# A planner's prices for TensorE, SyncE and shared VectorE/GpSimd time, and the instruction order that follows from them

## The chip, the cores and the metric

One core of a Trainium2 chip runs the whole program: TensorE (PE in the rows), VectorE (DVE), ScalarE (ACT), GpSimd (POOL), SyncE (SP, which here issues nearly all transfers) and 16 DMA engines. The metric is the device time of one execution in microseconds, the median of a few runs.

## The reference

Causal attention with a bias from cumulative sums, then two feed-forward blocks, all in fp32:

```python
scores = scale * np.matmul(q, k.transpose(0, 1, 3, 2))      # 4 x 8 heads, 576 x 576, depth 64
bias = -(cum[:, :, :, None] - cum[:, :, None, :])           # cum = cumsum(max(s, 0))
scores = np.where(causal, -1e9, scores + np.minimum(bias, 0.0))
...                                                         # softmax, then times v
x = attn_out  ->  2304 x 512
g = s * max(x @ w_in, 0) ** 2 + b                           # 512 -> 2048
x = g @ w_out                                               # 2048 -> 512
h = max(x @ w1, x @ w2, x @ w3)                             # 512 -> 768
out = h @ w_fin                                             # 768 -> 512
```

## The kernel before, in words

Attention is done in 20 jobs, one pair of heads each. Jobs 0 to 3 do the first 320 query rows of batch 0 (part "A"), 4 to 7 the other 256 rows of it ("B"), and jobs 8 to 19 a whole pair of heads ("W", 576 rows). A job is a chain of small steps: the scores of a block of query rows (`qk`, L571 and L573; in W jobs `qk_set`, L581, one head j at a time), their row minima on VectorE (`least`, L592), the exponential on ScalarE (`expo`, L598), its transposition on TensorE (`turn_p`, L670) and a copy out of PSUM (`copy_p`, L265 or L269), the product with v (`av`, L689), and the division by the row sums (`turn_r` L618, `spread_r` L660, `x_copy` L697).

In W jobs the operands of `qk_set` lie in a tile `set` (two of them, used in turn). It is filled by `round_set` (a rounded copy of q and k, 128 x 1152, on ACT or DVE), `rest_set` (what the rounding left out, in three pieces on POOL), `again_set`, and a transfer `decay_set` (L523, four rows from `dm_d`).

The first feed-forward block's first 6 of 16 hidden blocks run in the same stretch: the matmuls `mm` of L276 to L278 (three for each product, high and low parts) fill TensorE's time between attention steps as far as the finished jobs have given them input. Weights are converted on the way in (`weight_steps`: L301 issues the load, L306 on ACT, then L309 to L321 on DVE, ACT and POOL). From about 265 us on only feed-forward matmuls are left.

The order on every engine comes from a planner in the kernel (`Plan.order`), run as the program is built. Every step has a price per engine it may run on (`costs`), a due time (`prio`) and the steps that it needs. The planner always takes next what can begin first by its own clock; among what can begin within `SLACK` us of that, it takes the lowest due time. A step that may run on two engines goes to the second when the first would be done later than that by a margin (`LATE`, `LATE_F`, `LATE_0`). `LAND` and `FAR` are its allowances for a transfer's landing; `PORT` names DVE steps that it doesn't let overlap GpSimd's steps. What it writes down is a fixed order, in which each engine works one instruction after the other.

The step `keep` (L543) transposes the identity into a PSUM bank that nobody reads. It has the last due time of all, so that the planner puts it where TensorE would have nothing else.

Of the kernel before, what the change touches and what calls it, by code (L numbers as in the profile page):

```python
# [18 lines left out]
P = 128  # L19
BIG = 1.0e9  # L20
LO = 32
PARTS = 3
# [3 lines left out]
XS_BUFS = 2  # L26
ST2 = 3
COLD = 6.7
DM_AT = 47.138
DM_AFTER = ("dd", 2)  # L30
D_AT = -2.0
WARM = 30
KEEP = 1
KEEPS = 40
VIA = 8

WO = ((0, 1, 2), (3, 4, 5), (6, 7, 8, 9))
PACE_0 = 0
PACE_S = 1.381
F_AT = 15  # L40
F_PACE = 2.4

PER = {'A': 5.6, 'B': 9.085, 'W': 16.166}
Q_LOAD = -8.188
K_LOAD = -18.606
SET_AT = -5.4
V_LOAD = 3.528
TURN = -6.0
LEAST = 0.259
EXP = 0.52  # L50
D_T = 1.77
P_HI = 0.616
R_AT = 0.543
D_AV = 5.38
X_COPY = 0.345
X_HI = 2.019
X_LO = 2.696
AV = {"A": ((0, 1, 2),), "B": ((0, 1, 2), (3, 4)), "W": ((0, 1, 2), (3, 4))}
W_1 = -2.561
W_S1 = 3.438  # L60
W_2 = 28.48
W_S2 = 1.679
WG = (0, 1, 2, 5, 6)
WX = (7, 10, 13)
# [1 line left out]
WB_S = 8.964  # L66
WO_AT = 0.055
W_AT = (0, 2.0, 2.3, 2.8, 2.9, 3.3)
SLACK = 0.03
LATE = 0.898  # L70
LATE_F = 0.923
LATE_0 = 0.133
BUSY = 150
RATE = 1.022
RATE_D = 360e3
FAR_S = 0.306
FAR_R = 0.557
FAR_Q = 0.632
LOADED = (60, 260)
LOAD = {"ACT": RATE, "DVE": RATE}  # L80
LAND = {"wa": 1.1, "ws": 1.0, "wb": 1.1, "wf": 1.1, "q": 0.7, "k": 1.0, "v": 1.0, "decay": 0.7, "x_d": 0.7, "load_x": 0.7, "t": 1.1, "lw": 1.0, "ls": 1.0, "s_b": 0.6}
FAR = {"ws": FAR_S, "wa": FAR_S, "q": FAR_Q, "k": FAR_Q, "v": FAR_Q}
TAIL = {"least": 0.067, "inv": 0.085, "x_copy": 0.055, "relua": 0.06, "relub": 0.06, "copy_p": 0.045, "copy_r": 0.045}
MANUAL = lambda nc: {x.engine for x in (nc.tensor, nc.scalar, nc.vector, nc.gpsimd, nc.sync)}


class Plan:
# [8 lines left out]
             ("DVE", "ACT"): 0.13, ("DVE", "PE"): 0.17, ("DVE", "Pool"): 0.2, ("Pool", "PE"): 0.15, ("Pool", "DVE"): 0.15, ("Pool", "ACT"): 0.1}  # L96


    PORT = ("square", "lo", "hi", "x_hi", "x_lo", "xb_lo", "lo_h", "lo_y", "hl")
    OVERLAP = 0.1  # L100

    def __init__(self, rings):
# [10 lines left out]
    def order(self):  # L113
        n = len(self.steps)
        waits, users, needs = [0] * n, [[] for _ in range(n)], []
# [6 lines left out]
        free, start, end, engine = {}, [None] * n, [None] * n, [None] * n  # L122
# [54 lines left out]
        for i in range(n):  # L177
            if not waits[i]:
                make_ready(i)
        for done in range(n):  # L180
            best = None
            for e in ready:
                times = list(choices(e))
                if times:
                    limit = min(times)[0] + SLACK
                    b, p, i = min((x for x in times if x[0] <= limit), key=lambda x: (x[1], x[2]))
                    if best is None or b < best[0]:
                        best = (b, i, e)
            if best is None:
                raise RuntimeError(f"stuck after {done} of {n}: {[(self.steps[i][0]) for m in ready.values() for i in m][:40]}")  # L190
            t, i, e = best
            key, costs, prio, _, f, args, _, _ = self.steps[i]
            engine[i], start[i], end[i] = e, t, t + costs[e] * (2 if e == "PE" and t < COLD else LOAD.get(e, 1) if LOADED[0] < t < LOADED[1] else 1)
            free[e] = end[i] - (TAIL.get(key[0], 0) if e == "DVE" else 0)
            if has_port(i, e):
                port[e] = end[i]
            for o in costs:
                ready[o].remove(i)
            self.now = []
            for r, back in taken(i):  # L200
                z = min(range(len(held[r])), key=lambda z: given_back(held[r][z], e))
                held[r][z] = back
                self.now.append((r, z))
            for j in users[i]:
# [12 lines left out]
def fused_kernel(ctx, tc, q, k, v, s, w_in, w_out, ms, mb, w1, w2, w3, w_fin, out,  # L217
                 f_split=6):
    nc = tc.nc
    B, H, S = s.shape  # L220
# [528 lines left out]
    def add(key, engine, cost, prio, needs, f, *args, att=False, delay=None, **k):  # L749

        costs = engine if isinstance(engine, dict) else {engine: cost}
        if att and key[0] not in ("copy_rb", "load_rb", "x_copy", "x_hi", "x_lo"):
            attention.append(key)
        if engine == "SP":
            raw, kind = key[0] in ("q", "k"), key[0] + (key[1] if key[0] == "w" else "")
            plan.add(("issue", *key), {"SP": (0.6 if raw else 0.475) * cost[0] + 0.17 * (cost[0] // 3)}, prio, needs, f, *args, delay=0.65, **k)
            plan.add(key, {"DMA": 1.5 if key[0] == "s_b" else cost[1] * P * 4 / RATE_D}, prio, [("issue", *key)], lambda: None, delay=0.95 + LAND.get(kind, 0.4) + FAR.get(kind, 0) + (delay or 0))
            return
        plan.add(key, costs, prio, needs, f, *args, delay=delay, **k)
# [28 lines left out]
    for job in jobs:  # L788
# [33 lines left out]
        for x, u in enumerate(units):  # L822
            i, k0, k1, c0, c1 = UNITS[u]
            if pairs:
                same = [("turn_p", n - 1, z, j) for z in range(6) if UNITS[z][0] == i for j in range(2)]
                order = [("after", ("qk", n, units[x - 1]))] if x else [("after", z) for z in last_qk]
                ready = [("oh", n), ("q", n), ("k", n)]
                add(("qk", n, u), "PE", 5 * (k1 - k0) / 2400 + 0.25, at[u, 0], ready + [("dd", i)] + [("after", z) for z in same] + order, qk, job, u,
                    take=[("sm", [("least", n, u, j)]) for j in range(2)], **a)
            for j in range(2):  # L830
                same = [("turn_p", n - 1, z, j) for z in range(6) if UNITS[z][0] == i]
                if not pairs:
                    order = [("qk", n, units[x - 1], j)] if x else [("qk", n, units[-1], 0)] if j else last_qk
                    add(("qk", n, u, j), "PE", 2 * max(0.112, mm_cost(k1 - k0)) + 0.04, at[u, j], [("rest", n, j, z) for z in range(PARTS)] + [("again", n, j), ("decay", n, j)] + [("after", z) for z in same + order], qk_set, job, u, j,
                        take=[("sm", [("least", n, u, j)])], **a)
                add(("least", n, u, j), "DVE", dve(k1 - k0) + 0.08, at[u, j] + LEAST, [qk_key(n, u, j)] + same + ([("least", n, units[x - 1], j)] if k0 else []), least, job, u, j, **a)
        for i in job.chunks:
# [5 lines left out]
        by = lambda m: {"ACT": act_ps(m), "DVE": dve_ps(m)} if pairs else {"DVE": dve_ps(m), "ACT": act_ps(m)}  # L843
        freed = [("x_copy", n - z, hf) for z in range(1, NP + 2) for hf in range(2)]
        if spread:
            add(("turn_r", n), "PE", 0.109, end + R_AT + 0.5, [("inv", n)], turn_r, job, take=[("sm", [("copy_r", n), ("rest_r", n)])], **a)
            add(("copy_r", n), by(P), 0, end + R_AT + 0.5, [("turn_r", n)] + [("spread_r", n - 1, hf) for hf in range(2)], copy_r, job, **a)
            add(("rest_r", n), "DVE", dve_ps(P), end + R_AT + 0.5, [("copy_r", n)], rest_r, job, **a)
        else:
            add(("turn_r", n), "PE", 0.109, end + R_AT + 0.5, [("inv", n)], turn_r, job, take=[("sm", [("copy_r", n)])], **a)  # L850
            add(("copy_r", n), by(P), 0, end + R_AT + 0.5, [("turn_r", n), ("load_rb", n - 2), ("spread_r", n - 1, 0), ("spread_r", n - 2, 0)], copy_rw, job, **a)
            plan.add(("issue", "save_r", n), {"SP": 0.475 if pairs else 0.95}, end + R_AT + 0.6, [("copy_r", n)], save_r, job)
            plan.add(("save_r", n), {"DMA": 0.05}, end + R_AT + 0.6, [("issue", "save_r", n)], lambda: None, delay=1.2)
# [7 lines left out]
        for z, (u, j) in enumerate(turns):  # L861
# [6 lines left out]
                add(("turn_p", n, u, j), "PE", max(0.03, 0.109 * (c1 - c0) - 0.05), t, [("exp", n, i, j), ("pp",) if i > 2 else ("pre", "Pool")] + order, turn_p, job, u, j, take=[("sm", [("copy_p", n, u, j)])], **a)  # L868
# [7 lines left out]
                add(("copy_p", n, u, j), {"ACT": act_ps(m), "DVE": dve_ps(m)}, 0, t + P_HI, [("turn_p", n, u, j)] + over, copy_p, job, u, j, take=take, **a)  # L876

        t2 = end + D_AV
        for x, g in enumerate(job.groups):
            cost = 0.03 + sum(mm_cost(z, 4) + 0.05 for z in (HS[hf] + HN[hf] - max(c * P, HS[hf]) for c in g for hf in job.halves) if z > 0)  # L880
# [806 lines left out]
```

## Time and profile before

| | us |
|---|---|
| median of 3 runs | 876.33 (875.36 to 876.64) |
| the profiled execution | 873.61 |
| its span, first to last instruction | 871.7 |
| TensorE busy in it | 859.2 |
| VectorE, ScalarE, GpSimd busy | 642.4, 468.4, 342.5 |

The span is what the views below divide up; 1.9 us lie around it. "Busy" of TensorE counts pipelined matmuls from start to modelled end, so it shows where the engine has nothing to do, not how well it is used.

### The profile page before, as it was taken

To read this page: it belongs to the slowest core of one execution; us is meant where nothing else is said; L and a number is where in the kernel's file an instruction comes from. 1 tells how busy PE (TensorE), PEld (TensorE's weight loads), DVE (VectorE), ACT (ScalarE), POOL (GpSimd) and SP (SyncE) were. 2 spreads that over 40 slices of the span, in tenths; PEclk is the share of its full clock that TensorE was granted. 3 is DMA by queue.
4 is the path that set the end of the run, shared out by engine and by line. 5 is a ranking of instruction groups with operands and counts; after the bars stand their busy time and mean duration, and the time that the engine had idled before them with its cause. 6 is when DMAs were issued, how large, how long until landed. Compare 5 with 4: busy or idle time off the path is not lost.

```text
span 871.7 us, 15599 instructions
## 1 busy us (share of the span) xinstructions
PE 859.2 (99%) x5056; PEld 770.5 (88%) x5056; DVE 642.4 (74%) x1550; ACT 468.4 (54%) x1173; POOL 342.5 (39%) x367
## 2 busy tenths in 40 slices
PE   8999999999999999999999999999999999999998
PEld 7678888888888999999988888889999999989996
DVE  8889897989887877777979796444668366846650
ACT  7887998888883435536355452451235323432221
POOL 3334689767842322524142150420227222602220
PEclk9899999999999999999999999999999999999999
DMA  7645666676553456475859766329886255715501
GB/s 209 195 130 169 202 208 188 213 239 190 186 173 120 144 185 217 146 252 167 292 177 304 240 196 209 102 95 325 303 300 228 74 169 178 233 73 170 169 25 73
DMA packets 110672, 162.72 MB, mean 187 GB/s; under 512 B 10912, under 2 KB 61952, under 8 KB 110592
## 3 DMA queue, kind: packets, MB, share of 16 engines
q1 hardware_dynamic: 110352, 161.45, 57.2%
q8 instruction: 41, 0.67, 0.3%
q14 instruction: 39, 0.32, 0.1%
q10 hardware_dynamic: 240, 0.28, 0.1%
HBM read 117.26 MB, written 44.42 MB: 185 GB/s over the span
## 4 chain that ended last, share of the span: by engine, by line
PE 89%; DVE 5%; DMA 3%; ACT 1%; SPq 1%; issue 1%; DVEq 0%; ACTq 0%
PE mm L276 25%; PE mm L277 25%; PE mm L278 25%; PE pt L670 5%; PE px L689 4%; PE ps L581 4%; DVE pp L592 1%; PE ps L571 1%; DMA stage<-in_moe_w_out_dram 1%; DMA stage<-in_moe_w_in_dram 1%; ACT pp L598 1%; SPq L503 1%; DMA wst<-in_moe_w_in_dram 1%; DMA raw<-in_k_dram 1%; DMA set<-dm_d 0%
## 5 line engine op out<-in xcount | busy, mean ns | idle before, releaser
L272 POOL TENSOR_TENSOR gbl<-g,gbh 128x512 fp32r<-128x512 f32 (+1 forms) x50 | 64.2, 1285 | 141.2 <-ACT gbh L265 141.2
L1131 ACT ACTIVATE g<-g 128x512 f32<-128x512 f32 (+4 forms) x86 | 48.3, 561 | 81.8 <-DVE g L1127 81.3
L598 ACT ACTIVATE pp<-pp,mn 64x64 f32<-64x64 f32 (+4 forms) x160 | 88.3, 554 | 4.5 <-DVE mn L592 4.0
L272 POOL TENSOR_TENSOR set<-raw,set 64x384 fp32r<-64x384 f32 x72 | 76.4, 1084 | 30.1 <-ACT set L265 23.0
L276 PE MATMUL mm<-ty,sdp 128*128 128x384 f32 x252 | 84.2, 334 | 0.0
L277 PE MATMUL mm<-ty,sdp 128*128 128x384 f32 x252 | 84.2, 334 | 0.0
L278 PE MATMUL mm<-ty,sdp 128*128 128x384 f32 x252 | 84.2, 334 | 0.0
L1127 DVE TENSOR_SCALAR g<-mm 128x512 f32<-128x512 f32 (+4 forms) x86 | 51.7, 601 | 42.0 <-PE mm L278 41.5
L670 PE MATMUL pt<-ident,pp 128*128 128x128 f32 x480 | 78.2, 281 | 3.0 <-DVE mn L592 1.4
L278 PE MATMUL mm<-gbh,wb_out 128*128 128x512 f32 (+2 forms) x200 | 73.6, 368 | 0.0
L276 PE MATMUL mm<-gbh,wb_out 128*128 128x512 f32 (+2 forms) x200 | 73.6, 368 | 0.0
L277 PE MATMUL mm<-gbl,wb_out 128*128 128x512 f32 (+2 forms) x200 | 73.6, 368 | 0.0
L278 PE MATMUL mm<-xa,wb_in 128*128 128x512 f32 (+1 forms) x200 | 73.4, 367 | 0.0
L277 PE MATMUL mm<-xa,wb_in 128*128 128x512 f32 (+1 forms) x200 | 73.4, 367 | 0.0
L276 PE MATMUL mm<-xa,wb_in 128*128 128x512 f32 (+1 forms) x200 | 73.4, 367 | 0.0
L272 POOL TENSOR_TENSOR ga<-g,ga 128x448 fp32r<-128x448 f32 (+3 forms) x36 | 39.5, 1099 | 79.3 <-ACT ga L265 66.7
L670 PEld LDWEIGHTS pt<-ident,pp 128*128 128x128 f32 x480 | 56.5, 142 | 15.8 <-ACT pp L598 3.7
L592 DVE CUSTOM_DVE_ANT_0 pp<-late_keys,ps 64x64 f32<-64x64 f32 (+4 forms) x160 | 62.2, 418 | 8.4 <-PE ps L581 5.6
L265 ACT ACTIVATE pt<-pt 128x384 f32<-128x384 f32 (+3 forms) x154 | 61.5, 429 | 10.3 <-PE pt L670 9.3
L581 PE MATMUL ps<-set 128*128 128x288 f32 (+4 forms) x288 | 55.7, 316 | 1.9 <-DMA set<-dm_d 1.8
L689 PE MATMUL px<-pt,vn 128*64 128x256 f32 (+3 forms) x512 | 51.9, 344 | 0.0
L276 PE MATMUL mm<-ga,wa_out 128*128 128x448 f32 (+3 forms) x144 | 51.4, 357 | 0.0
(265 smaller groups left out, 2430.4 us busy)
## 6 DMA issues: line engine op xcount, KB each, us to landing
sdp<-s_d SPq DMA_DIRECT2D x126, 256.0 KB
s_d<-sdp SPq DMA_DIRECT2D x42, 384.0 KB
wst<-in_moe_w_dram SPq DMA_DIRECT2D x24, 384.0 KB
wst<-in_moe_w_out_dram SPq DMA_DIRECT2D x32, 256.0 KB
raw<-in_q_dram SPq DMA_DIRECT2D x24, 288.0 KB
raw<-in_k_dram SPq DMA_DIRECT2D x24, 288.0 KB
bl<-y_d SPq DMA_DIRECT2D x24, 192.0 KB
out_dram<-o SPq DMA_DIRECT2D x17, 256.0 KB
```

Of the source, the lines that this page charges most:

```text
L265: nc.scalar.activation(dst, src, AF.Copy, scale=1.0 if scale is None else scale)
L272: ENGINES[on].tensor_tensor(dst, a, b, op=ALU.subtract)
L276: nc.tensor.matmul(ps, lhs[0], rhs[0], start=first, stop=False)
L277: nc.tensor.matmul(ps, lhs[0], rhs[1], start=False, stop=False)
L278: nc.tensor.matmul(ps, lhs[1], rhs[0], start=False, stop=last)
L581: nc.tensor.matmul(ps[:, :k1 - k0], t[:, a, QS[i]:QS[i] + P], t[:, b, k0:k1], start=x == 0, stop=x == 1)
L592: nc.vector.tensor_tensor_reduce(out=pp[j][i][:n, k0:k1], in0=late_keys[:n, a:a + k1 - k0], in1=ps_.pop((job.n, u, j))[:n, :k1 - k0], scal ...
L598: nc.scalar.activation(p[:n, :w], p[:n, :w], AF.Exp, bias=mns[job.n, j][:n, i:i + 1], scale=-1.0, accum_out=sums[job.n % 2][:n, j, i:i + 1])
L670: nc.tensor.transpose(pt[:, c - c0, :], pp[j][i][:, c * P:(c + 1) * P], ident)
L689: nc.tensor.matmul(px_[job.n][hf][j * D:(j + 1) * D, a0 - h0:h1 - h0], vn[job.n % 2][:, c, j, :], columns(job, pr["p", job.n, j], c, c + 1 ...
L1127: nc.vector.tensor_scalar(st["g", f], st["u", f][:, :n], 0.0, None, op0=ALU.max)
L1131: nc.scalar.activation(st["g", f], st["g", f], AF.Square)
```

## The change

The planner's numbers are changed, and with them the order; the work itself stays the same but for the 40 unread transpositions, which go (`KEEPS` 40 to 0). The new prices: a transposition step costs 0.03 us less by itself, and 0.083 more is charged to the first TensorE step after transpositions that is none itself (`SWITCH`); `turn_r` falls from 0.109 to 0.03, `av` by 0.07; `qk_set` is priced by block. An issue of SyncE costs 0.44 or 0.52 in place of 0.475 or 0.6. `copy_p` on ACT costs 0.015 more. `round` joins `PORT`. Due times, margins and landing allowances have new values.

```diff
-DM_AT = 47.138
+DM_AT = 47.801
...
-KEEPS = 40
+KEEPS = 0
...
-PER = {'A': 5.6, 'B': 9.085, 'W': 16.166}
+PER = {'A': 5.6, 'B': 9.085, 'W': 16.375}
...
-FAR_S = 0.306
-FAR_R = 0.557
-FAR_Q = 0.632
+FAR_S = 0.503
+FAR_R = 0.667
+FAR_Q = 0.826
...
+SWITCH = 0.083
+TURNS = ("turn_p", "turn_r")
...
-    PORT = ("square", "lo", "hi", "x_hi", "x_lo", "xb_lo", "lo_h", "lo_y", "hl")
+    PORT = ("round", "square", "lo", "hi", "x_hi", "x_lo", "xb_lo", "lo_h", "lo_y", "hl")
...
-            engine[i], start[i], end[i] = e, t, t + costs[e] * (2 if e == "PE" and t < COLD else LOAD.get(e, 1) if LOADED[0] < t < LOADED[1] else 1)
+            cost = costs[e]
+            if e == "PE":
+                cost += SWITCH * (last_turn and key[0] not in TURNS)
+                last_turn = key[0] in TURNS
+            engine[i], start[i], end[i] = e, t, t + cost * (2 if e == "PE" and t < COLD else LOAD.get(e, 1) if LOADED[0] < t < LOADED[1] else 1)
...
-            plan.add(("issue", *key), {"SP": (0.6 if raw else 0.475) * cost[0] + 0.17 * (cost[0] // 3)}, prio, needs, f, *args, delay=0.65, **k)
+            plan.add(("issue", *key), {"SP": (0.52 if raw else 0.44) * cost[0] + 0.17 * (cost[0] // 3)}, prio, needs, f, *args, delay=0.65, **k)
```

What this does to the order is shown at three places. Line numbers of the changed kernel are 7 higher than before at these instructions.

The first is TensorE just after the first three score blocks of job 0. L670 (L677) transposes the exponentials (`pp_0` to `pp_2`, of head 0 and then head 1), L543 is the unread transposition. Before:

```order
L670 MATMUL pt<-ident,pp_0_150 128x128
L543 MATMUL warm<-ident 128x128 x2
L670 MATMUL pt<-ident,pp_0_155 128x128
L543 MATMUL warm<-ident 128x128 x10
L670 MATMUL pt<-ident,pp_1_151 128x128 x2
L543 MATMUL warm<-ident 128x128 x2
L670 MATMUL pt<-ident,pp_1_156 128x128 x2
L543 MATMUL warm<-ident 128x128 x17
L670 MATMUL pt<-ident,pp_2_152 128x128 x3
L670 MATMUL pt<-ident,pp_2_157 128x128 x3
```

Now:

```order
L677 MATMUL pt<-ident,pp_0_150 128x128
L677 MATMUL pt<-ident,pp_0_155 128x128
L677 MATMUL pt<-ident,pp_1_151 128x128 x2
L677 MATMUL pt<-ident,pp_1_156 128x128 x2
L677 MATMUL pt<-ident,pp_2_152 128x128 x3
L677 MATMUL pt<-ident,pp_2_157 128x128 x3
```

The twelve transpositions stand in the same order, with nothing between them; the other 9 of the 40 stood in the next 4 us of the program.

The second place is SyncE's queue in the first 15 us: L301 (L308) loads weights to convert, L529 and L531 load v, L503 loads q and k of job 2. Before:

```order
L301 DMA wg<-in_moe_w_in_dram 128x384
L301 DMA stage<-in_moe_w_in_dram 128x384
L529 DMA vn_118<-in_v_dram 128x2x128
L531 DMA vn_118<-in_v_dram 64x128
L503 DMA raw<-in_q_dram 64x320 x2
L503 DMA raw<-in_k_dram 64x320 x2
L301 DMA stage<-in_moe_w_in_dram 128x384
L301 DMA wst<-in_moe_w_in_dram 128x384
L529 DMA vn_117<-in_v_dram 128x2x128
```

Now:

```order
L308 DMA stage<-in_moe_w_in_dram 128x384
L536 DMA vn_118<-in_v_dram 128x2x128
L538 DMA vn_118<-in_v_dram 64x128
L308 DMA stage<-in_moe_w_in_dram 128x384
L510 DMA raw<-in_q_dram 64x320 x2
L510 DMA raw<-in_k_dram 64x320 x2
L308 DMA wst<-in_moe_w_in_dram 128x384
L308 DMA wg<-in_moe_w_in_dram 128x384
L536 DMA vn_117<-in_v_dram 128x2x128
```

The second `stage` load moved ahead of q and k; the `wst` load is still the eighth transfer after the first `stage` load.

The third place is TensorE ahead of the first scores of job 12, the ninth use of a `set` tile (128x64, the last row). Before, from the last score block (288 columns) of job 11:

```order
L581 MATMUL ps<-set 128x288 x2
L276 MATMUL mm<-xhi,wa_in 128x256
L277 MATMUL mm<-xlo,wa_in 128x256
L278 MATMUL mm<-xhi,wa_in 128x256
L670 MATMUL pt<-ident,pp_2_157 128x128 x3
L276 MATMUL mm<-xhi,wa_in 128x256
L277 MATMUL mm<-xlo,wa_in 128x256
L278 MATMUL mm<-xhi,wa_in 128x256
L581 MATMUL ps<-set 128x64 x2
```

Now (the rows left out hold five more threes of `mm` and 11 transpositions):

```order
L588 MATMUL ps<-set 128x288 x4
L283 MATMUL mm<-xhi,wa_in 128x256
L284 MATMUL mm<-xlo,wa_in 128x256
L285 MATMUL mm<-xhi,wa_in 128x256
...
L283 MATMUL mm<-ga,wa_out 128x258
L284 MATMUL mm<-ga,wa_out 128x258
L285 MATMUL mm<-ga,wa_out 128x258
L677 MATMUL pt<-ident,pp_3_158 128x128 x4
L588 MATMUL ps<-set 128x64 x2
```

Between the two jobs' scores TensorE had 2 threes of `mm` and 3 transpositions; now it has 7 threes and 15 transpositions.

Counted over the whole program, 7 in place of 14 of the 24 large roundings (128 x 1152) are on DVE, 17 in place of 10 on ACT; 16 in place of 12 of `again_set` are on POOL. The number of `mm` threes ahead of the last `turn_r` is 149 where it was 139. SyncE issues the same transfers.

## Rows read from the trace of the kernel before

**Rows 1.** Busy time by stretch: start:end length, engines, TensorE's granted clock, DMA.

```profile
7.10:22.80 15.70, 13.33 (x113) 10.53 (x112) 14.60 (x54) 14.81 (x49) 1.02 (x5) 1.00 0.86 264
22.83:29.64 6.81, 6.74 (x35) 4.59 (x35) 3.97 (x18) 4.95 (x19) 2.98 (x3) 0.50 0.53 157
60.00:265.00 205.00, 201.53 (x1566) 171.35 (x1566) 179.33 (x582) 177.79 (x524) 137.49 (x150) 1.00 0.61 192
265.00:850.00 585.00, 585.00 (x3024) 542.67 (x3024) 411.72 (x795) 238.78 (x493) 183.30 (x168) 1.00 0.57 189
```

**Rows 2.** TensorE's waits, whole span: us in total, times, longest.

```profile
PE ps L581 <- DMA set<-dm_d: 1.8, 1, 1.8
...
PE pt L670 <- DVE mn L592: 1.4, 3, 1.0
PE pr L660 <- DVE rt L652: 0.9, 1, 0.9
PE ps L571 <- ACT pt L265: 0.7, 1, 0.7
...
PE pt L670 <- DMA wg<-in_moe_w_in_dram: 0.3, 1, 0.3
```

**Rows 3.** Unread transpositions (L543) and those at the start (L537): ns min/median/max, starts.

```profile
L543 PE MATMUL warm<-ident x40: 272/273/329, 10.4 to 18.5; 128*128 128x128 f32 x40
...
L537 PE MATMUL warm<-ident x30: 273/421/476, 1.7 to 6.9; 128*128 128x128 f32 x30
```

**Rows 4.** Timeline of TensorE, 12 to 29 us: start, length.

```profile
12.51 2.02 PE L543 MATMUL warm<-ident 128*128 128x128 f32 x17
14.36 0.82 PE L670 MATMUL pt<-ident,pp 128*128 128x128 f32 x6
...
16.59 1.20 PE L689 MATMUL px<-pt,vn 128*64 128x320 f32 x12
...
23.57 1.54 PE L670 MATMUL pt<-ident,pp 128*128 128x128 f32 x6
...
26.55 2.19 PE L689 MATMUL px<-pt,vn 128*64 128x320 f32 x12
```

**Rows 5.** Timeline of ScalarE, 13 to 20 us, with idle time ahead in brackets.

```profile
13.22 0.55 ACT L598 ACTIVATE pp<-pp,mn 128x320 f32<-128x320 f32 x1
...
20.02 0.55 ACT L306 ACTIVATE stage<-wst 128x384 f32<-128x384 f32 x1 [0.89 <-DMA wst<-in_moe_w_in_dram]
```

**Rows 6.** The chain of waits, 9 to 20 us: start, length.

```profile
9.48 5.78 DMA stage<-in_moe_w_in_dram
...
15.28 4.72 DMA wst<-in_moe_w_in_dram
```

**Rows 7.** Timeline of TensorE, 136 to 140 us.

```profile
136.84 0.28 PE L276 MATMUL mm<-xhi,wa_in 128*128 128x256 f32 x1
...
137.20 0.49 PE L670 MATMUL pt<-ident,pp 128*128 128x128 f32 x3
137.45 0.36 PE L276 MATMUL mm<-xhi,wa_in 128*128 128x256 f32 x1
...
137.89 0.19 PE L581 MATMUL ps<-set 128*128 128x64 f32 x1
139.92 0.30 PE L581 MATMUL ps<-set 128*128 128x64 f32 x1 [1.84 <-DMA set<-dm_d]
```

**Rows 8.** Timeline of SyncE, the `decay_set` of job 12's first head.

```profile
135.56 0.48 SPq L523 DMA_DIRECT2D set<-dm_d  x1
```

**Rows 9.** Instructions that fill `set`: ns min/median/max, starts, forms.

```profile
L265 ACT ACTIVATE set<-raw x22: 680/684/1169, 76.9 to 239.1; 64x576 fp32r<-64x576 f32 x12, 128x1152 fp32r<-128x1152 f32 x10
L269 DVE CAST set<-raw x14: 746/980/1573, 98.0 to 244.0; 128x1152 fp32r<-128x1152 f32 x14
```

**Rows 10.** First use and load of the second weights `wb_in`.

```profile
L276 PE MATMUL mm<-xa,wb_in x200: 334/389/390, 350.9 to 569.9; 128*128 128x512 f32 x60, 128*128 128x384 f32 x40
...
L1213 SPq DMA_DIRECT2D wb_in<-wb_d x12: 523/524/610, 300.8 to 339.1; - x12
```

More of the change, by code (lines that the diff above doesn't have):

```diff
@@ L28 @@
 COLD = 6.7
-DM_AT = 47.138
+DM_AT = 47.801
 DM_AFTER = ("dd", 2)
-D_AT = -2.0
+D_AT = -1.202
 WARM = 30
 KEEP = 1
-KEEPS = 40
+KEEPS = 0
 VIA = 8
@@ L38 @@
 PACE_0 = 0
-PACE_S = 1.381
+PACE_S = 1.466
 F_AT = 15
 F_PACE = 2.4
-PER = {'A': 5.6, 'B': 9.085, 'W': 16.166}
+PER = {'A': 5.6, 'B': 9.085, 'W': 16.375}
 Q_LOAD = -8.188
 K_LOAD = -18.606
-SET_AT = -5.4
-V_LOAD = 3.528
+SET_AT = -5.542
+V_LOAD = 5.472
 TURN = -6.0
-LEAST = 0.259
+LEAST = -0.111
 EXP = 0.52
@@ L55 @@
 X_COPY = 0.345
-X_HI = 2.019
-X_LO = 2.696
+X_HI = 2.273
+X_LO = 3.631
 AV = {"A": ((0, 1, 2),), "B": ((0, 1, 2), (3, 4)), "W": ((0, 1, 2), (3, 4))}
@@ L60 @@
 W_S1 = 3.438
-W_2 = 28.48
+W_2 = 29.555
 W_S2 = 1.679
@@ L68 @@
 W_AT = (0, 2.0, 2.3, 2.8, 2.9, 3.3)
-SLACK = 0.03
+SLACK = 0.044
 LATE = 0.898
-LATE_F = 0.923
+LATE_F = 0.805
 LATE_0 = 0.133
@@ L179, in order @@
                 make_ready(i)
+        last_turn = False
         for done in range(n):
@@ L833, in fused_kernel @@
                     order = [("qk", n, units[x - 1], j)] if x else [("qk", n, units[-1], 0)] if j else last_qk
-                    add(("qk", n, u, j), "PE", 2 * max(0.112, mm_cost(k1 - k0)) + 0.04, at[u, j], [("rest", n, j, z) for z in range(PARTS)] + [("again", n, j), ("decay", n, j)] + [("after", z) for z in same + order], qk_set, job, u, j,
+                    add(("qk", n, u, j), "PE", 2 * max(0.112, mm_cost(k1 - k0)) + (-0.08, 0.06, 0.02, 0.0, 0.0, 0.0)[u], at[u, j], [("rest", n, j, z) for z in range(PARTS)] + [("again", n, j), ("decay", n, j)] + [("after", z) for z in same + order], qk_set, job, u, j,
                         take=[("sm", [("least", n, u, j)])], **a)
@@ L845, in fused_kernel @@
         if spread:
-            add(("turn_r", n), "PE", 0.109, end + R_AT + 0.5, [("inv", n)], turn_r, job, take=[("sm", [("copy_r", n), ("rest_r", n)])], **a)
+            add(("turn_r", n), "PE", 0.03, end + R_AT + 0.5, [("inv", n)], turn_r, job, take=[("sm", [("copy_r", n), ("rest_r", n)])], **a)
             add(("copy_r", n), by(P), 0, end + R_AT + 0.5, [("turn_r", n)] + [("spread_r", n - 1, hf) for hf in range(2)], copy_r, job, **a)
@@ L849, in fused_kernel @@
         else:
-            add(("turn_r", n), "PE", 0.109, end + R_AT + 0.5, [("inv", n)], turn_r, job, take=[("sm", [("copy_r", n)])], **a)
+            add(("turn_r", n), "PE", 0.03, end + R_AT + 0.5, [("inv", n)], turn_r, job, take=[("sm", [("copy_r", n)])], **a)
             add(("copy_r", n), by(P), 0, end + R_AT + 0.5, [("turn_r", n), ("load_rb", n - 2), ("spread_r", n - 1, 0), ("spread_r", n - 2, 0)], copy_rw, job, **a)
@@ L867, in fused_kernel @@
                 m = (c1 - c0) * QN[i]
-                add(("turn_p", n, u, j), "PE", max(0.03, 0.109 * (c1 - c0) - 0.05), t, [("exp", n, i, j), ("pp",) if i > 2 else ("pre", "Pool")] + order, turn_p, job, u, j, take=[("sm", [("copy_p", n, u, j)])], **a)
+                add(("turn_p", n, u, j), "PE", max(0.03, 0.109 * (c1 - c0) - 0.08), t, [("exp", n, i, j), ("pp",) if i > 2 else ("pre", "Pool")] + order, turn_p, job, u, j, take=[("sm", [("copy_p", n, u, j)])], **a)
                 over, take = [("after", ("copy_p", n, units[0], j))], []
@@ L875, in fused_kernel @@
                     take = [("ph" if n < 2 * NP else "p", [("av", n, g) for g in job.groups])]
-                add(("copy_p", n, u, j), {"ACT": act_ps(m), "DVE": dve_ps(m)}, 0, t + P_HI, [("turn_p", n, u, j)] + over, copy_p, job, u, j, take=take, **a)
+                add(("copy_p", n, u, j), {"ACT": act_ps(m) + 0.015, "DVE": dve_ps(m)}, 0, t + P_HI, [("turn_p", n, u, j)] + over, copy_p, job, u, j, take=take, **a)
         t2 = end + D_AV
         for x, g in enumerate(job.groups):
-            cost = 0.03 + sum(mm_cost(z, 4) + 0.05 for z in (HS[hf] + HN[hf] - max(c * P, HS[hf]) for c in g for hf in job.halves) if z > 0)
+            cost = -0.04 + sum(mm_cost(z, 4) + 0.05 for z in (HS[hf] + HN[hf] - max(c * P, HS[hf]) for c in g for hf in job.halves) if z > 0)
             order = [("after", ("av", n, job.groups[x - 1]))] if x else [("after", ("av", n - 1, jobs[n - 1].groups[-1]))] if n else []
```

## The prediction

> **What bounds the kernel now.** I read busy time by stretch first. From 265 to 850 us TensorE has 585.00 of 585.00 us busy at a granted clock of 1.00, while DVE, ACT and POOL have room [rows 1]. No order of steps shortens that stretch, since its matmuls are the same afterwards. Between 60 and 265 us TensorE has 201.53 of 205.00, so at most 3.5 us of plain idle time lie there; DVE (179.33) and ACT (177.79) are 87% busy, close enough that a step in the wrong place is felt. Before 30 us things differ: from 7.10 to 22.80 ACT (14.81 of 15.70) and DVE (14.60) set the pace, and from 22.83 to 29.64 TensorE is busy for 6.74 of 6.81 us at a clock of 0.50, which is the lower of its two levels, 1.2 GHz [rows 1].
>
> Next the waits of TensorE. After the start there are eight kinds; the five rows shown add up to 5.1 us, and the three left out lie between 0.3 and 0.5 each, so some 6.3 us in all [rows 2]. The largest is one wait of 1.8 us for a transfer into `set`. With the half clock, which costs half of 6.74 = 3.4 us of TensorE's time, these are about all that a new order can win: not quite 10 us of 873.61, the profiled execution's own time. It lies 2.7 us under the median of 876.33, so I work out a difference against 873.61 and lay it on the median.
>
> **The change part by part.**
>
> *The wait before job 12's scores.* TensorE came to this `qk_set` at 137.89 and got the four decay rows at 139.92 [rows 7]. Their transfer had been issued at 135.56 [rows 8], 4.4 us before. The scores before it had left TensorE 2 threes of `mm` and 3 transpositions to do; in the new order it has 7 threes and 15 transpositions there. A three takes 0.36 us (136.84 to 137.20), three transpositions 0.25 (137.20 to 137.45) plus 0.08 that shows in the next `mm` (0.44 from 137.45 to 137.89 against 0.36) [rows 7]. So the gap grows from about 1.1 to 7 x 0.36 + 5 x 0.33 = 4.2 us, and the wait should be mostly covered. The bounds are 0 (the transfer is issued later too, since it stands behind two loads of v which wait for an earlier product) and -1.84. I take **-1.5**, near the full amount, because the cover grew by more than the wait. What is late next is the rest of `set` for the same job, made by POOL; I keep 0.3 us for it.
>
> *The 40 unread transpositions.* They took TensorE time in which it mostly had nothing else, so their 40 x 0.11 us are not a gain. They cost something only where real work stood behind them. The plainest place: the 17 from 12.51 run to the start of six real ones at 14.36 [rows 4], while the exponential that those wait for ended at 13.77 [rows 5]. That leaves 0.6 us, less some 0.2 to hand over. I take **-0.4**; the bounds are 0 (ACT copies these blocks later anyway) and -1.85, the whole run (12.51 to 14.36).
>
> *The clock.* The row shows 1.00 up to 22.80 and 0.50 from 22.83 to 29.64 [rows 1]. At the start TensorE ran only the 30 transpositions of L537: they took 421 ns by median and 273 at the least, so the clock rose among them; the unread ones later took 273 too [rows 3]. Transpositions thus let the clock rise and kept it up. Without the 40, TensorE has twelve short transpositions from about 10 to 14.5 us where it had 43, so the clock probably falls earlier. The price of half clock is in the rows: six transpositions take 1.54 in place of 0.82 us, the first `px` product 2.19 in place of 1.20 [rows 4]. For those twelve and one product that is 1.4 + 1.0 = 2.4 us, the upper bound. But ACT sets the pace there, and if TensorE is busier for being slower, the clock may be up again before 22.8, and the 3.4 us of the later stretch are not lost: the lower bound is -3.4. Between the two I take **+0.3**: the first product is a little later, and the low stretch moves more than it grows. The Trainium skill ("TensorE: Matmul & The Clock Gate", Part 4) says that a transposition does not count as activity for the clock in the way that a matmul does. By that the 40 had no part in the clock and this term would be 0; rows 3 speak against it.
>
> *The stall on `wst`.* ACT lost 0.89 us at 20.02 until this load had landed, with the exponentials of job 1 behind it [rows 5]. SyncE could issue the load only at 15.28, as the first `stage` load landed (9.48 + 5.78 = 15.26) eight transfers earlier, and it took 4.72 us [rows 6]. In the new queue `wst` is again eighth behind that load. I take 0; the bounds are -0.89 and +0.9 (as much again, since the second `stage` load now travels ahead of it).
>
> *Roundings.* Seven large roundings go from DVE (0.98 us median, from 0.746 up to 1.573) to ACT (1.17, the longest of its row), and four `again_set` from ACT (0.68) to POOL [rows 9]. DVE is relieved of 6.9 us, ACT gets 8.2 - 2.7 = 5.5. In the stretch of 205 us that makes 172 and 183: both still under TensorE's 201.53, which hides it. Without that cover it would cost up to 5.5 us over twelve jobs. I take 0.
>
> *Prices of TensorE's steps, `SWITCH` among them.* They change no instruction's duration. Three transpositions and what shows behind them make 0.25 + 0.08 = 0.33 us, about 3 x 0.11 [rows 7]; a change of kind costs nothing beyond that. I count no gain for fewer such changes.
>
> *Everything else in the order.* The other 4.5 us of waits are dealt anew. The new prices sit closer to the pitches of rows 7, so I expect slightly fewer: **-0.4**. The bounds are -3 (two thirds vanish) and +3 (two thirds as much again is added).
>
> The sum is -1.5 - 0.4 + 0.3 - 0.4 = **-2.0 us**: 871.6 for a profiled execution, and 874.3 against the median of 876.33.
>
> **The rivals.** A measurement of this kernel can tell about 0.2% from no change, which is 1.75 us; the forecast is just past it.
>
> *Redrawn, not removed.* A fixed order meets durations that no plan knows: roundings on DVE run from 0.746 to 1.573 us [rows 9]. Then each wait that goes is replaced elsewhere. For it: seven of the eight kinds are single waits of under 1 us, which looks like chance; against it: the largest has a cause that the order removes. Time: 876.3, give or take 1.
>
> *The clock is low twice (slower).* Without the 40 the clock falls before 15 us, rises, and falls again near 22.8 because the work there is as sparse as before. Then the +2.4 come on top of the 3.4 already lost, and the gain of -0.4 goes as DVE and ACT wait for TensorE. If the wait at job 12 is then also merely moved, the time is 876.33 + 2.4 = 878.7. It decides from a low clock of some 11 us in the first 40, against 6.8 now. For it: TensorE's idle time ahead of the first products; against it: ACT is the slower engine there.
>
> *Transpositions don't count for the clock.* Then the clock's term is 0 and the sum -2.3: 874.0. (This is the rule of the Trainium skill's page named above.) Rows 3 make it unlikely.
>
> *The later end of attention.* Ten more threes stand ahead of the last `turn_r`. At 448 columns one takes about 0.63 us (an estimate: 0.36 us at 256 columns [rows 7] times 448/256), so the conversion of later weights starts some 6 us later. First load of `wb_in` at 300.8, first use at 350.9 [rows 10]: 50 us of cover. I give this no chance of its own.
>
> **How the numbers follow.** Forecast 0.45, redrawn 0.30, clock low twice 0.20, transpositions not counting 0.05. Of the forecast's 0.45, 0.38 lie beyond 0.2%, and of "redrawn" 0.02; with the 0.05 that makes faster 0.45. Same: 0.07 + 0.25 + 0.02 = 0.34. Slower: 0.03 + 0.18 = 0.21. The range goes from 871.5 (the clock's stretch moves to where ACT hides it, -3.4, and the rest of the sum falls short) to 878.7 (clock low twice). Inside the forecast alone I would say 872.3 to 875.5.
>
> **What would show it.** In the changed kernel's profile: TensorE's wait for `set<-dm_d` under 0.5 us; the sum of its waits after the start near 4.5 us; one stretch of half clock of about 7 us before 30 us, perhaps earlier; ACT still waiting about 0.9 us for `wst`; 585 of 585 us busy after 265. I am wrong if the clock is low for much more than 7 us, if a new wait of over 1 us shows in TensorE's list, or if the first product `px` begins later than 17.5 us (16.59 now).

## The result, and the profile after

| | before | after |
|---|---|---|
| median | 876.06 (874.17 to 877.33, 6 runs) | 867.50 (866.47 to 869.81, 6 runs) |
| profiled execution | 873.61 | 868.97 |
| its span | 871.7 | 867.2 |

The ratio is 0.9907 (0.9889 to 0.9925): 0.93% faster. The forecast was 874.3, range 871.5 to 878.7. The sign was right; the time lies 4 us below the range. When the two kernels ran again on two other chips (below), the gain was 5.7 and 6.3 us in place of 8.6; that too is more than the 4.8 that the range allowed.

First busy time by stretch in the changed kernel: the time, TensorE, its weight loads, VectorE, ScalarE, GpSimd, the granted clock, the DMA share and GB/s (against [rows 1]).

```profile
7.10:15.30 8.20, 3.97 (x27) 2.57 (x26) 7.35 (x28) 8.20 (x28) 0.86 (x5) 1.00 0.93 306
15.31:28.96 13.65, 13.60 (x66) 9.35 (x66) 11.05 (x42) 10.76 (x39) 2.34 (x3) 0.50 0.64 186
60.00:265.00 205.00, 204.95 (x1593) 175.61 (x1592) 178.00 (x592) 182.13 (x523) 129.73 (x145) 1.00 0.62 194
265.00:850.00 585.00, 585.00 (x3017) 541.27 (x3018) 405.11 (x797) 238.58 (x490) 179.04 (x164) 1.00 0.58 189
```

Three things are to be seen. From 265 us on TensorE is busy for 585 of 585 us, as before. From 60 to 265 us TensorE was idle for 3.47 of 205 us before and is now for 0.05, while its weight loads grew from 171.35 to 175.61 us: more work fits into the same stretch. At the start the stretch at half clock (1.2 of 2.4 GHz) is 13.65 us long in place of 6.81, and begins 7.5 us earlier.

TensorE's waits over the whole span (answers [rows 2]): us in total, times, longest.

```profile
PE pt L677 <- ACT pt L272: 2.8, 1, 2.8
...
PE pt L677 <- DVE mn L599: 1.0, 1, 1.0
PE ps L580 <- POOL pp L564: 0.2, 1, 0.2
PE ps L578 <- DVE mn L599: 0.2, 1, 0.2
```

The wait for `set<-dm_d` has no row any more, and these four all lie before 30 us. In the chain that ended last (the page's part 4: shares of the span by engine) the first line is before, the second now:

```profile
PE 89%; DVE 5%; DMA 3%; ACT 1%; SPq 1%; issue 1%; DVEq 0%; ACTq 0%
PE 98%; DVE 1%; ACT 1%; DMA 0%; issue 0%; ACTq 0%; DVEq 0%
```

The timeline of TensorE at the start (answers [rows 4]; start, length, and idle time ahead in brackets):

```profile
10.43 1.51 PE L677 MATMUL pt<-ident,pp 128*128 128x128 f32 x6 [0.95 <-DVE mn L599]
14.72 1.02 PE L677 MATMUL pt<-ident,pp 128*128 128x128 f32 x6 [2.78 <-ACT pt L272]
...
16.98 1.34 PE L696 MATMUL px<-pt,vn 128*64 128x320 f32 x4
...
28.16 1.69 PE L696 MATMUL px<-pt,vn 128*64 128x320 f32 x12
```

Between the two groups of six real transpositions, where 17 unread ones stood, TensorE has nothing to do. The second six wait for a copy out of PSUM on ScalarE, not for the exponential. ScalarE's own timeline there (answers [rows 5]; the first line is from the kernel before):

```profile
13.77 0.57 ACT L265 ACTIVATE pt<-pt 128x64 f32<-128x64 f32 x3
...
13.32 0.55 ACT L605 ACTIVATE pp<-pp,mn 128x320 f32<-128x320 f32 x1
...
14.47 0.83 ACT L272 ACTIVATE pt<-pt 128x64 f32<-128x64 f32 x4
...
20.71 0.23 ACT L272 ACTIVATE pt<-pt 128x64 f32<-128x64 f32 x1 [1.44 <-PE pt L677]
20.83 0.56 ACT L313 ACTIVATE stage<-wst 128x384 f32<-128x384 f32 x1
```

The exponential ends at 13.87 (13.77 before), the four copies that free the bank begin at 14.47, and the six start at 14.72, 0.36 us later than with the unread ones ahead of them (14.36). In the kernel before, such copies ran right behind the exponential and ended at 14.34; now two other steps of ScalarE come first. ScalarE no longer waits for `wst` at 20.83; just ahead of it, it waits 1.44 us for TensorE, which runs at half clock.

The last row is the first use of `wb_in`, behind which the two kernels do the same work (answers [rows 10]; min/median/max ns, first and last start):

```profile
L283 PE MATMUL mm<-xa,wb_in x200: 334/389/390, 346.3 to 565.3; 128*128 128x512 f32 x60, 128*128 128x384 f32 x40
```

It was 350.9 before. These 4.6 us are the whole difference of the two profiled executions (873.61 - 868.97 = 4.64), and from there to the end the span has 520.8 and 520.9 us. So the gain is made before 346 us.

### The profile page after: what moved, and what is told of

Read it like the earlier page. It is cut to its first block, busy times and chain, and to the rows that moved or that the text cites. A ratio compares the mean times of both kernels' runs of the same rounds, so it can differ in the third digit from the quotient of the medians.

```text
span 867.2 us, 15482 instructions
## 1 busy us (share of the span) xinstructions
PE 857.3 (99%) x5016; PEld 767.7 (89%) x5016; DVE 635.8 (73%) x1561; ACT 473.0 (55%) x1167; POOL 333.0 (38%) x362
## 4 chain that ended last, share of the span: by engine, by line
PE 98%; DVE 1%; ACT 1%; DMA 0%; issue 0%; ACTq 0%; DVEq 0%
PE mm L283 26%; PE mm L284 26%; PE mm L285 26%; PE pt L677 7%; PE px L696 6%; PE ps L588 5%; PE ps L578 2%; PE pr L625 0%; PE ps L580 0%; PE pr L667 0%; DMA s<-in_s_dram 0%; ACT s L555 0%; DVE s L382 0%; DVE pp L599 0%; ACT pt L272 0%
## 5 line engine op out<-in xcount | busy, mean ns | idle before, releaser
L279 POOL TENSOR_TENSOR set<-raw,set 64x384 fp32r<-64x384 f32 x72 | 73.4, 1043 | 35.9 <-ACT set L272 25.6
L677 PE MATMUL pt<-ident,pp 128*128 128x128 f32 x480 | 77.1, 281 | 4.0 <-ACT pt L272 2.8
L677 PEld LDWEIGHTS pt<-ident,pp 128*128 128x128 f32 x480 | 56.7, 142 | 15.3 <-ACT pp L605 5.1
L272 ACT ACTIVATE pt<-pt 128x256 f32<-128x256 f32 (+3 forms) x151 | 60.9, 433 | 16.4 <-PE pt L677 13.9
L588 PE MATMUL ps<-set 128*128 128x288 f32 (+4 forms) x288 | 53.3, 313 | 0.0
```

The costliest lines, as they stand in the source:

```text
L272: nc.scalar.activation(dst, src, AF.Copy, scale=1.0 if scale is None else scale)
L279: ENGINES[on].tensor_tensor(dst, a, b, op=ALU.subtract)
L588: nc.tensor.matmul(ps[:, :k1 - k0], t[:, a, QS[i]:QS[i] + P], t[:, b, k0:k1], start=x == 0, stop=x == 1)
L677: nc.tensor.transpose(pt[:, c - c0, :], pp[j][i][:, c * P:(c + 1) * P], ident)
```

## The experiments

The theories that the expectations name: **pitches** (the new prices of TensorE's steps match what the chip takes, and so the written order holds), **one order** or **bad drawing** (any touch draws another order, some are lucky), **clock** (unread transpositions keep TensorE's clock up), **unread** (they cost TensorE time on the path). Each ratio is to the kernel before on the same chip, whose median was 873.6 to 874.8 there.

### Prices and constants apart

Three kernels without unread transpositions: the kernel before otherwise; the new prices with the old due times, margins and allowances; the old prices with the new ones.

```diff
# first
-KEEPS = 40
+KEEPS = 0
# second: the first, and all prices of the change (SWITCH, PORT, costs, issues)
# third: the first, and all constants of the change (DM_AT ... FAR_Q)
```

> The kernel before with the 40 unread transpositions left out (KEEPS 0) and nothing else changed. Theory 'prices': the gain of the change comes from TensorE's lost time between 60 and 265 us, which new prices remove; leaving the transpositions out alone leaves those waits and adds half clock (13.6 us in the changed kernel's profile against 6.8), so 876 to 880. Rival 'unread': they held real work up, and leaving them out is the gain: 868 to 871. Rival 'one order': any new order meets other waits, 873 to 879.

> The changed kernel with all due times, margins and landing allowances of before: new prices of steps, PORT with round, no unread transpositions. 'Prices': most of the gain stays, 868 to 871. 'Constants' (the gain is in the new due times, margins and allowances): back to 874 to 877. 'One order' (the gain belongs to this one order alone): 873 to 877 too.

> The kernel before with all new due times, margins and landing allowances and no unread transpositions, but the old prices and PORT. 'Prices': waits of TensorE stay about as before, 873 to 878. 'Constants': 867 to 870. 'One order': 873 to 877.

| | us | ratio |
|---|---|---|
| neither | 874.48 | 1.0006 (0.9989 to 1.0022) |
| prices alone | 871.17 | 0.9966 (0.9950 to 0.9981) |
| constants alone | 872.49 | 0.9979 (0.9961 to 0.9998) |
| both: the changed kernel, three times | 867.50, 868.67, 868.54 | 0.9907, 0.9929, 0.9922 |

Against "neither", prices are worth 0.40%, constants 0.27%, both 0.77 to 0.99%: about the sum, or a little over it. Neither half carries the gain by itself. None of the theories had all three ranges right: "prices" expected 876 to 880 for the first, "one order" 873 to 877 for the second, "constants" 867 to 870 for the third.

These medians hide something. Runs of one kernel differ in TensorE's granted clock over the span (1.000 is full speed throughout), and the time goes with it (next section), so like should be set beside like. The runs with a mean clock of 0.987 to 0.992 took, by mean, 874.6 us with neither (11 runs), 871.6 with prices alone (8), 874.1 with constants alone (4), and 868.8 to 869.1 with both (10 runs on three chips). At like clock prices are worth 3.0 us, constants at most some 0.5, and both some 5.6: clearly more than the sum.

Nor does the ratio of 1.0006 say that the 40 made no difference in the kernel before. Without them the planner drew another order: TensorE's real steps differ from the 29th on, and the wait for `set<-dm_d` is 0.3 us in place of 1.8. The highest mean clock in its 12 runs is 0.996, while 11 of 29 runs of the kernel before had 1.000. Those of the kernel before with a low clock (0.991 to 0.993, 5 runs) took 877.1 us by mean, against the 874.6 above. So a lower clock and a better order cancelled each other there.

### The changed kernel with its 40 unread transpositions

```diff
-KEEPS = 0
+KEEPS = 40
```

> The changed kernel with the 40 unread transpositions put back. 'Clock': they hold the clock up until they run out, the half-clock stretch shrinks from 13.6 to about 6.8 us, and the time falls to 864 to 867. 'Unread': the time rises by 1 to 4 us, since real steps stand behind them. If neither matters: 867.5 within 1.

865.19 (865.05 to 867.76), ratio 0.9903 (0.9879 to 0.9927). The changed kernel did not run on this chip, so it was repeated beside it:

> The changed kernel once more, so that the next three stand beside it on one chip. All theories: ratio to before 0.990 to 0.994, 867 to 869, one or two stretches of half clock before 31 us, 13 to 17 us together, and a TensorE that is busy for over 204.5 of the 205 us from 60 to 265.

> The changed kernel with the 40 unread transpositions put back, beside the changed kernel on one chip. Up to 265 us its order on TensorE is the changed kernel's but for those 40. Theory 'clock': they keep the clock at 1.00 where it was 0.50 for 13 to 17 us, and each 6.8 us of half clock was worth 1.5 to 1.8 us in the timed runs, so it is 2 to 4 us faster than the changed kernel (864.5 to 866.5) with no or one stretch of half clock. Theory 'unread' (their 4.4 us of TensorE time are on the path): 1 to 4 us slower than the changed kernel. Theory 'transpositions do not count for the clock': half clock as in the changed kernel and the same time within 0.7 us.

The changed kernel took 868.54 (866.89 to 868.95; 0.9922), the one with the 40 took 865.41 (864.94 to 865.75; 0.9891, 0.9872 to 0.9909). The ranges don't overlap: the 40 are worth 3.1 us. But for them, the order of instructions is the same on every engine, so nothing else can be the cause. Its stretches:

```profile
7.10:60.00 52.90, 50.61 (x387) 37.92 (x386) 49.89 (x168) 49.36 (x154) 18.97 (x25) 1.00 0.68 203
60.00:265.00 205.00, 204.95 (x1585) 176.83 (x1584) 175.22 (x585) 180.02 (x516) 128.76 (x144) 1.00 0.61 193
```

The granted clock is 1.00 in the first stretch, where the changed kernel has 0.87 in the profiled execution above and 0.94 in the one on this chip. (In the changed kernel's three profiles half clock lasted 13.65, 17.07 and 6.83 us; the last, on this chip, is less than the 13 to 17 expected.) On TensorE the unread ones stand where it had nothing:

```profile
11.72 3.22 PE L550 MATMUL warm<-ident 128*128 128x128 f32 x28
14.78 0.82 PE L677 MATMUL pt<-ident,pp 128*128 128x128 f32 x6
...
16.73 1.08 PE L696 MATMUL px<-pt,vn 128*64 128x320 f32 x7
```

The six real ones behind them start at 14.78 (14.72 without) and take 0.82 in place of 1.02 us. "Clock" holds, "unread" falls. The runs say the same over the whole execution: the 17 of the changed kernel have mean clocks of 0.988 to 0.996, never 1.00; of the ten with the 40, nine have 0.999 or 1.000, and the tenth, at 0.996, is the 867.76 above. In the first six runs of the changed kernel the time follows the clock: 866.47 and 866.62 at 0.996, 867.94 and 868.97 at 0.992, 869.81 at 0.988.

This also lets the order be weighed at equal clock. On the chip of the three kernels without unread transpositions, 11 runs of the kernel before and 5 with the new order and the 40 had a clock of 1.000: 872.48 us by mean (871.30 to 873.51) against 865.15 (865.05 to 865.23). The order alone is worth 7.3 us.

### Twice as many

```diff
-KEEPS = 0
+KEEPS = 80
```

> 80 unread transpositions in the changed kernel in place of none. Theory 'clock': with 40 the clock was already at 1.00 throughout in most runs, so 80 give nothing more than 40 (within 1 us of it), and cost only where they delay real work: 0 to +1.5 us against 40. Theory 'unread': 40 more cost as much again, 1 to 4 us above 40. Theory 'clock, not yet full' (the one run with 40 that was low for some us shows it): up to 1 us below 40.

870.41 (868.53 to 870.61), ratio 0.9948 (0.9932 to 0.9964): 5 us more than with 40, more than any theory said. The clock is at 1.00, so that is not it.

```profile
7.10:60.00 52.90, 51.59 (x414) 39.12 (x414) 49.52 (x168) 48.69 (x152) 15.31 (x21) 1.00 0.67 203
60.00:265.00 205.00, 203.10 (x1581) 175.10 (x1578) 175.47 (x581) 180.71 (x519) 128.39 (x144) 1.00 0.60 191
```

From the 68th of the real matmuls on its order is another, and 1.9 us of idle time are back after 60 us. How the 5 us divide between the 40 further transpositions (4.4 us at 0.11) and the new order stays open.

### Three prices taken back, one at a time

The changed kernel was repeated, and in it were put back: all old prices of TensorE's steps; `round` outside `PORT`; the old issues of SyncE.

```diff
# first: prices of TensorE
-SWITCH = 0.083
+SWITCH = 0.0
# and turn_p, turn_r, av, qk_set, copy_p as before
# second
-    PORT = ("round", "square", ...
+    PORT = ("square", ...
# third
-(0.52 if raw else 0.44)
+(0.6 if raw else 0.475)
```

> The changed kernel once more, so that the next three are compared with it on the same chip. All theories: ratio to before 0.989 to 0.993, some 865 to 868. 'Clock': its runs spread over 3 us or more, in steps, as the half-clock stretch lasts for about 7, 14 or 20 us.

> The changed kernel with TensorE's old prices alone (no SWITCH, old prices of turn_p, turn_r, av, qk_set, and copy_p without the 0.015). 'Pitches' (TensorE's prices are what makes the order fit): 3 to 6 us slower than the changed kernel, with 4 to 8 us of lost TensorE time between 60 and 265. 'One order': likewise 3 to 6 us slower, so this one tells little by itself, but with the next two: 'pitches' wants it alone to be slow.

> The changed kernel without round in PORT, all else as changed. 'Pitches': within 1.5 us of the changed kernel. 'Port' (roundings on DVE that meet GpSimd's steps delay the path): 2 to 5 us slower, more than 7 roundings on DVE, with some over 1.1 us long. 'One order': 3 to 6 us slower.

> The changed kernel with SyncE's old prices of an issue (0.475 and 0.6). 'Pitches' and 'port': within 1.5 us of the changed kernel. 'One order': 3 to 6 us slower, since the smallest change of a price gives another order.

| | us | ratio |
|---|---|---|
| changed kernel | 868.67 | 0.9929 (0.9905 to 0.9954) |
| old prices of TensorE | 873.17 | 0.9986 (0.9967 to 1.0004) |
| `round` not in `PORT` | 870.09 | 0.9950 (0.9929 to 0.9971) |
| old issues of SyncE | 869.60 | 0.9947 (0.9930 to 0.9964) |

All three draw another order, from the 60th, the 402nd and the 19th of TensorE's 4682 matmuls on. Two of them keep most of the gain; that with TensorE's old prices loses 4.5 of 5.7 us. For the `PORT` and the issue the intervals still touch that of the changed kernel, so 1.4 and 0.9 us are not certain. In runs with a clock of 0.994 to 0.996 the four took 867.35, 872.48, 869.45 and 869.05 us by mean (2, 7, 5 and 5 runs): 5.1, 2.1 and 1.7 us lost, the last two a little more than "pitches" allowed. Of the "4 to 8 us of lost TensorE time" that it expected with the old prices, 1.35 us show as idle time from 60 to 265 us.

### Are those 4.5 us a bad drawing?

A nudge of two constants in the changed kernel, then the same nudge on the old prices, and the old prices in two halves.

```diff
# changed kernel nudged
-PER = {'A': 5.6, 'B': 9.085, 'W': 16.375}
+PER = {'A': 5.6, 'B': 9.085, 'W': 16.35}
-LEAST = -0.111
+LEAST = -0.1
# half one: SWITCH, turn_p and turn_r as before; half two: av and qk_set as before
```

> The changed kernel with one due-time constant (PER of W, 16.375 to 16.35) and one margin (LEAST, -0.111 to -0.1) nudged: a new order with the same prices. Theory 'pitches': the prices carry the gain, so at most 2 us above the changed kernel (867 to 870), TensorE busy for at least 204 of 205 us from 60 to 265. Theory 'one order' (the gain belongs to one lucky drawing): 3 to 6 us above it (871 to 874), TensorE busy for 202 to 203.7 there.

> The changed kernel with only the old prices of the transpositions: SWITCH 0, turn_p 0.03 dearer, turn_r at 0.109. Theory 'neighbour' (charging what shows behind a transposition to the next step of another kind is what lets the plan hold): 3 to 5 us above the changed kernel (871 to 873.5), TensorE busy for under 204 of 205 us from 60 to 265. Theory 'product and scores' (the prices of av and qk_set carry it): within 1.5 us of the changed kernel (867 to 870), over 204.3 busy.

> The changed kernel with only the old prices of av (0.07 dearer) and qk_set (0.04 for every block). Theory 'neighbour': within 1.5 us of the changed kernel (867 to 870), over 204.3 of 205 us busy. Theory 'product and scores': 3 to 5 us above it (871 to 873.5), under 204 busy.

> All old prices of TensorE in the changed kernel again, with the nudge that left the changed kernel's time as it was (PER of W 16.35, LEAST -0.1): a second drawing with the old prices. Theory 'pitches' (the old prices cost time in any drawing): 871 to 875, TensorE busy for under 204 of 205 us from 60 to 265, waits of TensorE there of 2 us or more. Theory 'bad drawing' (the first run with old prices was unlucky): 867 to 870.

The nudged kernel took 867.89 (0.9919, 0.9902 to 0.9936), 0.65 us below its partner. Half one took 871.93 (0.9967, 0.9952 to 0.9983), half two 869.61 (0.9946, 0.9929 to 0.9963): most of the loss goes with the transpositions and what is charged behind them, as "neighbour" said, though it also wanted TensorE busy for over 204.3 of the 205 us in half two, which had 203.00. The fourth took 873.51 (0.9990), but with the old prices this nudge leaves every engine's order as it was; so it was only the first order again, and told nothing of another drawing. Three more were run:

```diff
# old prices of TensorE, second drawing: PER of W 16.4, LEAST -0.15
# old prices of TensorE, third drawing: PER of W 16.32, SLACK 0.04
# new prices, the nudge of the third drawing
```

> The changed kernel with all old prices of TensorE and a small nudge of two due-time numbers (PER of W 16.4, LEAST -0.15), which draws an order that parts from the first one with old prices at the 66th matmul. (The nudge of the run before this one left that order as it was, so that run was the same order once more.) Theory 'pitches' (old prices cost time in any drawing): 871 to 875, TensorE busy for under 204 of 205 us from 60 to 265. Theory 'bad drawing' (the first order with old prices was unlucky): 867 to 870, over 204 busy.

> A third drawing with the old prices (PER of W 16.32, SLACK 0.04), another order from the 587th matmul on. Theory 'pitches': 871 to 875, under 204 of 205 us busy. Theory 'bad drawing': 867 to 870, over 204 busy.

> The changed kernel (new prices) with the same nudge as the run before (PER of W 16.32, SLACK 0.04), as its partner on one chip: another order from the 682nd matmul on. Theory 'pitches': at most 2 us above the changed kernel (867 to 870.5) and at least 2 us below the old prices with this nudge. Theory 'bad drawing': anywhere between 867 and 874, as often above its partner as below.

| order | old prices of TensorE | new prices |
|---|---|---|
| first | 873.17 and 873.51 (0.9986, 0.9990) | 867.50 to 868.67 (0.9907 to 0.9929) |
| other | 874.08 (0.9992, 0.9978 to 1.0005) | 867.89 (0.9919, 0.9902 to 0.9936) |
| same nudge | 870.05 (0.9953, 0.9935 to 0.9972) | 867.61 (0.9927, 0.9910 to 0.9944) |

The drawing counts: the third order with old prices is 3 to 4 us better than the others, and better than "pitches" allowed by 1 us. But in this table three orders with the new prices lie within 1.2 us, below every one with the old prices, and of the two with the same nudge on one chip the new prices are 2.4 us lower. Three kernels above have TensorE's new prices as well: those with the old constants, with `round` outside `PORT` and with the old issues. Their medians (871.17, 870.09, 869.60) are hardly better than the best drawing with old prices, 870.05, or worse. At like clock the two groups part: runs at 0.994 to 0.996 took, by mean, 866.7 to 869.6 us in the six orders with TensorE's new prices, and 870.0 (a single run, of the kernel "neither") to 873.4 in five with the old ones, with 875.0 to 875.8 in the kernel before. The second drawing with old prices, in TensorE's waits from 60 to 265 us:

```profile
PE pt L677 <- ACT pp L605: 1.0, 3, 0.4
PE pr L625 <- DVE rr L621: 0.9, 1, 0.9
PE pt L677 <- ACT stage L313: 0.7, 1, 0.7
PE pt L677 <- ACT pt L272: 0.4, 1, 0.4
PE ps L588 <- DVE mn L599: 0.3, 1, 0.3
```

Its busy time in that stretch:

```profile
60.00:265.00 205.00, 201.68 (x1567) 170.69 (x1567) 177.07 (x582) 179.59 (x529) 123.99 (x139) 1.00 0.61 192
```

The third order with the new prices has one wait of TensorE there, and this busy time:

```profile
PE pt L677 <- ACT wbs L272: 0.6, 1, 0.6
```

```profile
60.00:265.00 205.00, 204.42 (x1583) 174.69 (x1580) 174.38 (x578) 183.92 (x524) 123.88 (x139) 1.00 0.61 192
```

The first is like the kernel before (201.53 us busy there, five kinds of waits), the second like the changed kernel. In both, the waits are for engines that are under 90% busy: what is missing is not their time but that a step is ready when TensorE comes to it. That the right pitches tell the planner when that is remains argued, but that they are right can be seen. The time from one TensorE step's start to the next one's, 60 to 265 us, can be set against what the planner reckoned with. With TensorE's old prices the two differ by 0.040 to 0.043 us by median, in all six orders; with the new ones by 0.007, in all six. In sum nothing is mended: over these 205 us TensorE falls behind the planner's clock by 10.5 us both in the kernel before and in the changed one. So what sets the two apart is the single step, not the total.

## Why the forecast was wrong, point by point

**The step that failed** is the term "Everything else in the order": -0.4 us with bounds of 3 on either side. It measured about -5.5: at equal clock the order is worth 7.3 us, of which the wait before job 12 is 1.8. Beside it stood the sentence on the prices, "I count no gain for fewer such changes", which looked only at whether there would be fewer changes of kind. TensorE's prices were worth 2.4 us (same nudge) to 4.5 us (all else equal) in the pairs on one chip, or 3.1 to 5.1 at a clock of 0.994 to 0.996. The rest of the 5.5 lies in the constants and the other prices together, and in the luck of the drawing; how it divides stays open.

The size was bounded too low because the bound came from idle time. The forecast counted 6.3 us of waits in [rows 2] (the eight kinds add up to 6.5, and five of them, not seven, are single waits of under 1 us), and 3.47 us of idle time from 60 to 265 us. But [rows 7] show that three transpositions are busy for 0.49 us while the next matmul starts after 0.25: the end of one step lies 0.24 us over the beginning of the next. A wait shorter than that shows as no idle time, and a longer one costs up to 0.24 more than its bracket. Worked out from the starts of TensorE's steps instead (each step's time to the next start, less the usual pitch of its kind and shape, by a fit over all steps), the time lost from 60 to 300 us falls by 5 to 7 us, depending on how the pitches are fitted. That is an estimate, but it comes nearer to the 7.3 of the runs than the 3.4 of the idle rows. The Trainium skill says that matmul busy time is not a good measure of how near a kernel is to its limit, since matmuls are pipelined ("Perfetto Trace Analysis", Identifying the Most-Contended Engine); this case agrees, with 3.4 us by idle time against 7.3 by the runs.

**The wait before job 12's scores**: -1.5 forecast; the row is gone, which is its -1.84. The trace bears out the mechanism. The transfer's issue in the changed kernel:

```profile
134.31 0.48 SPq L530 DMA_DIRECT2D set<-dm_d  x1
```

Behind job 11's scores, from 134.49 on, TensorE has other work for 4.05 us, where 4.2 were forecast, and it comes to the rows of this transfer at 138.54, 4.2 us after their issue, without a wait. The gap is particular to this order: with `round` outside `PORT` a wait for `set<-dm_d` of 0.9 us at the longest is back.

**The 40 unread transpositions**, -0.4: wrong, it is nothing. I took the exponential's end (13.77) for what the second six waited for; it was ScalarE's copies behind it, which ended at 14.34, just ahead of the six at 14.36. With the 40 put back into the changed kernel the six start at 14.78, without them at 14.72.

**The clock**, +0.3 with bounds of +2.4 and -3.4: the sign was right and the size was not; putting the 40 back gained 3.1 us, more than the upper bound. The low stretch came earlier, as I wrote, but it also stayed low through the first products, 13.65 us. The rival "The clock is low twice" had the length right (13.65 us, where it wanted some 11), but it is one stretch and not two; its ScalarE waiting for TensorE is there (1.44 us). It gave the wrong time because the order won more. That taking the 40 out of the kernel before cost nothing by the median (ratio 1.0006) does not speak against the clock, since the order changed there too.

**The rival "Transpositions don't count for the clock"** falls. With the same order on every engine but for the 40, the clock is 1.00 with them and 0.50 for 6.83 to 17.07 us without. The Trainium skill ("TensorE: Matmul & The Clock Gate", Part 4) says that a transposition does not count as busy time for the clock in the usual way; these runs, with fp32 transpositions, contradict it.

**The stall on `wst`**, 0: the 0.89 us are gone, and a wait of 1.44 for TensorE stands ahead; for the end of the kernel the term was right to be small. **Roundings**: VectorE and ScalarE from 60 to 265 us are at 178.00 and 182.13 against forecast 172 and 183, under TensorE's 204.95; hidden as said.

**"Redrawn, not removed"**, to which I gave 0.30, falls for the new prices: nudged orders keep the gain. Yet it describes the old prices well, whose drawings differ by 4 us. Merely leaving out the 40 drew a better order from the old prices, which its low clock then hid.

Of what was to be seen, the sum of waits "near 4.5 us" came out at 4.2, but these waits now lie before 30 us where ScalarE sets the pace; the wait of over 1 us that was to show me wrong is among them, and harmless. Of my three signs of being wrong, two came, this wait and a clock low for much more than 7 us; but the forecast failed by the order, which was none of them.

A version better than both kernels came out of it: the changed one with its 40 unread transpositions, 865.19 and 865.41 us, 0.97 to 1.09% faster than before.

## What to carry to other kernels

When an order is planned ahead, check the planner's price of each step against the start-to-start pitch in the trace, by kind and by what stands next to it; prices that missed by 0.04 us a step on the engine that bounds the kernel cost it 2.4 to 4.5 us of 870. The sum tells less: TensorE fell behind the plan by 10.5 us in the slower kernel and in the faster. A kernel with one thing left out can be another order throughout: compare the orders before calling its time the price of that thing. Don't take the idle time of a pipelined engine as the bound of what a better order can win; take starts of steps, or runs at equal clock. Work that nobody reads may earn its place where the engine would idle at the start and lose its clock: here 40 transpositions of 0.11 us gave back 3.1 us.

## What the runs showed of the hardware that was not expected

TensorE's clock fell to 1.2 GHz at 15.31 us, after a stretch of 8.20 us in which it was busy for 3.97, and rose again at 28.96, after 13.65 us in which it was busy for 13.60. With the 28 unread transpositions from 11.72 to 14.78 us it stayed at 2.4 GHz. Between runs of one program the mean clock of the span went from 0.988 to 0.996, and the time from 869.81 to 866.47 with it, so single runs of such a kernel are best compared at equal clock.
